# One preLN GFNet + GEGLU kernel: Newton steps for up to four blocks at a time, block 15 folded on VectorE, and another list for the first stage

## The chip, the cores and the metric

The kernel runs on one core of a Trainium2 chip. The metric is the device time of one execution in microseconds (us), as the median of several runs.

## The reference

```python
def reference(A_x, A_w_r, A_w_i, B_x, B_w_gate, B_w_up, B_w_down):
    x = A_x                                            # 1 x 2048 x 512
    h = x + irfft2(rfft2(layernorm(x)) * (A_w_r + 1j * A_w_i))
    n = layernorm(h)
    return h + (gelu(n @ B_w_gate) * (n @ B_w_up)) @ B_w_down   # 512 -> 1376 -> 512
```

`layernorm` subtracts the mean over the last axis and divides by sqrt(variance + 1e-5). `A_w_r` and `A_w_i` are 2048 x 257. Everything is float32.

## The kernel before, in words

The 2048 rows are held as 16 blocks of 128 partitions x 512 columns, in the tile `gh`. The work goes in stages: a first stage of the Fourier transform over the rows, a second stage (transform over the columns, multiplication by `w`, and the first part of the way back), the end of the inverse transform with the second layer norm, and then the gated products, which take most of the time. All run on one core, and every engine takes its instructions in the order in which they are queued.

The change lies in the first stage. For every block b it does this, and the letters are those of the list `START`, which gives the order on each engine:

- `s`, `g`: mean and variance by bn_stats and bn_aggr on VectorE; for some odd blocks `m`, `q` instead, mean and sum of squares on ScalarE.
- `r`: rs = 1/sqrt(var + eps) by a ScalarE table. Beside it VectorE writes var + eps into the scratch `tmp`, which lies in PSUM.
- `n`: one Newton step on `rs`, three small VectorE instructions.
- `c`: ScalarE scales the block's cosine and sine table `mfs` by `rs` into `ms`. So the norm's division goes into the weights of the matmuls.
- `f`: GpSimd folds the columns of a group of one or two blocks: difference and sum of the two halves of a row, into `pn`, two instructions.
- `v` (`fold2`) and `u` (`sums2`): differences `uv` and sums `us` of the halves of `pn`. Where a block has no `u`, TensorE adds its two halves by one more matmul for each.
- `a`, `b`: `transform`, the matmuls of the block: components 0 and 1 from `pn` or `us`, components 2 and 3 from `uv`. An f32 matmul shows as two TensorE instructions.
- `k`, `l`: the block's spectrum is copied from PSUM to `ts`, by ScalarE or, for half of block 15, by VectorE.

Blocks are grouped as in `GROUPS`: 0 and 1 alone, six pairs, 14 and 15 alone. `r` and `n` go by group, but 14 and 15 together. Block 15's `f`, `u` and `v` are on GpSimd (`ON_POOL`). Fourteen small matmuls ahead of the stage warm TensorE up.

The second stage (`SECOND`) begins with `over_d`, whose matmuls (L413) read all 16 blocks of `ts`, so that it cannot begin before the first stage's last copy. Its other steps are `filtered` (multiplication by `w`) and `back`. The sums and differences `wh` of the edge columns of `w` are made on GpSimd and scaled by ScalarE; `patch_w` puts them into the tiles of `w`. `prep` prepares the gate and up weights (L199 and what follows) and its first GpSimd instruction waits for the last VectorE `fold2` (`lasts`).

The order of each engine inside one list is that of the list. Instructions of different lists (such as the edge sums, which stand behind `START` in the text) are put in order by a planner that runs when the kernel is built, by what it takes to be ready; `tc.issue_after(kept.ins)` names `kept`, the last ScalarE copy of the first stage, and queues what its block holds behind it.

Of the kernel before, what the change touches and what calls it, by code (L numbers as in the profile page):

```python
# [16 lines left out]
ALU = mybir.AluOpType  # L17
# [3 lines left out]
P = 128  # L21
NB = 16
# [3 lines left out]
EPS = 1e-5  # L26
# [5 lines left out]
BY_THEN = (8, 12, 9)  # L32

START = """
s0 g0 r0 s1 n0 g1 r1 f0 c0 a0 f1 s2 s3 g2 m5 f2 f4 f6 f8 g3 s4 n1 r2 q5 g4 c1 n2 a1 r4 v0 c2 a2 b0 c3 n4 m7 s6 v1 c4
c5 a4 g6 q7 m9 s8 v2 r6 g8 a3 b1 n6 q9 a5 s10 b3 m11 r8 c6 c7 k0 q11 b2 a6 g10 n8 a7 v4 c8 b4 b5 k1 a8 f10 f12 m13 k2
c9 a9 s12 v6 b6 b7 f14 r10 f15 u15 k3 g12 q13 n10 c10 c11 a10 m15 v8 b9 k4 a11 r12 k6 v10 k7 k5 b11 n12 b8 c12 s14 g14
q15 v12 c13 r14 k9 n14 b10 k10 k11 a12 c14 c15 u14 v14 v15 k8 a13 b13 k13 b12 a14 b14 k12 k14 a15 b15 l15 k15
"""

ON_POOL = (15,)

FIRST = """
u0.1 u4.0 w4 C4.0 V4.2 X4 w0 C0.1 V0.3 X0 U1.2 C1.4 V1.0 X1 r0 U5.3 C5.5 V5.1 M4.1 O4.0 M0.2 O0.1 U2.3 H4 H0 X5 C2.5
# [69 lines left out]
def kernel(  # L114
# [16 lines left out]
    pe, act, dve, pool = nc.tensor, nc.scalar, nc.vector, nc.gpsimd  # L131
# [6 lines left out]
    ident = base.tile([P, P], F32, name="ident")  # L138
# [4 lines left out]
    mv = base.tile([P, NB, 2], F32, name="mv")  # L143
# [18 lines left out]

    ps = ctx.enter_context(tc.tile_pool(name="ps", bufs=1, space=PSUM)).tile([P, 8, 512], F32, name="ps")

    for _ in range(14):

        pe.matmul(ps[:, 6, :P], ident, ident, start=True, stop=True)

    k3 = ctx.enter_context(tc.tile_pool(name="k3", bufs=1))
    dis = k3.tile([P, 4, P], F32, name="dis")  # L170
    mis = k3.tile([P, NB, P], F32, name="mis")
# [16 lines left out]
    def load_gu(f, slowly=False, after=None, by=None, raw=None):  # L188

        nonlocal turn  # L190
        t = raw() if raw else wgp.tile([P, 7, 2 * P], F32, name="raw")
        nc.sync.dma_start(t[:, :2], wgu[f, :, :2])
        nc.sync.dma_start(t[:, 3:6:2], wgu[f, :, 2:])
        r = gus[:, turn]
        turn = 1 - turn
        gu[f] = r.rearrange("p h m (c n) -> p h m c n", c=2)
        yield
        with held("late"):
            pooled["raw"] = i = pool.tensor_tensor(t[:, 4], t[:, 0], t[:, 3], op=ALU.subtract)  # L199
        if after:  # L200
            behind(i, after())
        yield
        pool.tensor_tensor(t[:, 3], t[:, 3], t[:, 5], op=ALU.add)
        yield
        pool.tensor_tensor(t[:, 2], t[:, 3], t[:, 0], op=ALU.subtract)
        yield
        pool.tensor_tensor(t[:, 6], t[:, 1], t[:, 2], op=ALU.subtract)
        yield
        if slowly:
            for m in range(7):  # L210
                split(r[:, 0, m], r[:, 1, m], t[:, m], pool)
                yield
        else:
            if not by:
                dve.tensor_copy(r[:, 0], t)  # L215
                yield
            for m in (slice(0, 1), slice(1, 4), slice(4, 7)):
                if by:
                    by.activation(r[:, 0, m], t[:, m], AF.Copy)
                pooled["lo"] = pool.tensor_tensor(r[:, 1, m], t[:, m], r[:, 0, m].bitcast(F32), op=ALU.subtract)  # L220
                yield
# [5 lines left out]
    with (  # L227
# [9 lines left out]
        rs = cp.tile([P, NB], F32, name="rs")  # L237
# [12 lines left out]
        group = {b + i: (b, n) for b, n in GROUPS for i in range(n)}  # L250
# [15 lines left out]
        def load_w(t):  # L266
            wts[t] = wtp.tile([P, 2, 2, NQ], F32, name="wt")
            nc.sync.dma_start(wts[t], w[t])

        ws = cp.tile([P, 2, NT, 2, 2, 2], F32, name="ws")  # L270
# [28 lines left out]
            act.activation(jk, gh[:, b], AF.Square, scale=D**-0.5, bias=m4[:, b : b + 1], accum_out=mv[:, b, 1:])  # L299


        tmp = ps[:, 7].rearrange("p (b k) -> p b k", b=NB)

        def root(b):

            n = group[b][1] if b < 14 else 2
            act.activation(rs[:, b : b + n], mv[:, b : b + n, 1], AF.Abs_reciprocal_sqrt, bias=eps)
            dve.tensor_scalar(tmp[:, b : b + n, 0], mv[:, b : b + n, 1], EPS, None, op0=ALU.add)

        def newton(b):  # L310

            n = group[b][1] if b < 14 else 2
            r, (ve, t) = rs[:, b : b + n], (tmp[:, b : b + n, k] for k in range(2))
            dve.scalar_tensor_tensor(t, r, -0.5, ve, op0=ALU.mult, op1=ALU.mult)
            dve.tensor_tensor(t, t, r, op=ALU.mult)
            dve.scalar_tensor_tensor(r, t, 1.5, r, op0=ALU.add, op1=ALU.mult)

        mss, pns, parts = {}, {}, {b: [None] * 4 for b in range(NB)}
# [5 lines left out]
        def fold(b):  # L324
            n = group[b][1]
            xv = gh[:, b : b + n].rearrange("p b (e n) -> p b e n", e=2)
            pn = pns[b] = w1.tile([P, 2, 2, 2, P], F32, name="pn", bufs=7)[:, :n]
            pv = pn.rearrange("p b e h n -> p b e (h n)")
            pool.tensor_tensor(pv[:, :, 1], xv[:, :, 0], xv[:, :, 1], op=ALU.subtract)  # L329
            pool.tensor_tensor(pv[:, :, 0], xv[:, :, 0], xv[:, :, 1], op=ALU.add)  # L330
            for i in range(n):
                parts[b + i][:2] = [[pn[:, i, 0, 0], pn[:, i, 0, 1]], [pn[:, i, 1, 0], pn[:, i, 1, 1]]]

        def fold2(b):
# [3 lines left out]
            uv = w1.tile([P, 2, 2, P], F32, name="uv", bufs=3)[:, :n]  # L338
            eng = pool if b in ON_POOL else dve
            i = eng.tensor_tensor(uv, pn[:, :, :, 0], pn[:, :, :, 1], op=ALU.subtract)  # L340
# [5 lines left out]
        def sums2(b):  # L346
            pn = pns[group[b][0]][:, b - group[b][0]]
            us = w1.tile([P, 2, P], F32, name="us", bufs=5)
            eng = pool if b in ON_POOL else dve
            eng.tensor_tensor(us, pn[:, :, 0], pn[:, :, 1], op=ALU.add)  # L350
            parts[b][:2] = [[us[:, 0]], [us[:, 1]]]

# [20 lines left out]
        def keep_half(b):  # L373
# [5 lines left out]
            "m": mean,  # L379
            "q": square,  # L380
            "r": root,
            "n": newton,
            "c": scale,
            "f": fold,
            "v": fold2,
            "u": sums2,
            "a": lambda b: transform(b, (0, 1)),
            "b": lambda b: transform(b, (2, 3)),
            "k": keep,
            "l": keep_half,  # L390
        }
        et = mybir.EngineType
        with tc.manual_schedule(engines={et.PE, et.Activation, et.DVE, et.Pool}):
            for op in START.split():
                kept = steps[op[0]](int(op[1:]))
            odd = slice(5, 16, 2)
            dve.tensor_scalar(mv[:, odd, 0], m4[:, odd], -(D**0.5), None, op0=ALU.mult)


# [2 lines left out]
        wh = cp.tile([P, NT, 2, 2, 2], F32, name="wh")  # L402
# [5 lines left out]
        def over_d(t, k):  # L408

            pd = ps[:, k : k + 2]  # L410
            for c, (e, q) in enumerate(((0, 0), (1, 1), (0, 1), (1, 0))):
                o = pd[:, e, q * NQ // 2 : (q + 1) * NQ // 2]
                pe.matmul(o, ts[:, t, c].rearrange("p x b k -> p (x b k)"), dfs[:, c], start=True, stop=True)  # L413
            pdv = pd[:, :, :NQ].rearrange("p e (s q) -> p s e q", s=2)
            dps[t] = w2.tile([P, 2, 2, NQ // 2], F32, name="dp", bufs=5)
            for h, d in ((slice(0, 64), 1), (slice(64, P), -1)):
                act.activation(dps[t][h], pdv[h, ::d], AF.Copy)  # L417
# [42 lines left out]

        with tc.manual_schedule(engines={et.PE, et.Activation, et.DVE, et.Pool}):
            prep = itertools.chain(raw0, load_gu(1, True))
            for m, op in enumerate((ALU.add, ALU.subtract)):
                pool.tensor_tensor(wh[:, :, m], ws[:, 0, :, m], ws[:, 1, :, m], op=op)
            with tc.issue_after(kept.ins):
                act.activation(wh, wh, AF.Copy, scale=0.5)
            for _ in range(4):
                next(prep)
            rounded = 0
            for op in SECOND.split():  # L470
                name, *place = op.split(".")
                t = int(name[1:] or 0)
                if name == "h":
                    for _ in range(2 if rounded == 6 else 1):
                        next(prep, None)
                    rounded += 1
                elif name[0] == "o":
                    over_d(t, int(place[0]))
                elif name[0] == "f":
                    filtered(t)  # L480
                    if t + AHEAD < NT:
                        load_w(t + AHEAD)
                else:
                    (patch_w if name[0] == "p" else back)(t)
# [3 lines left out]
    w3 = ctx.enter_context(tc.tile_pool(name="w3", bufs=2, reuse_waits="tile"))  # L488
# [928 lines left out]
```

## Time and profile before

| | |
|---|---|
| median of 3 runs | 441.16 us (440.86, 441.16, 442.53) |
| the profiled execution | 440.67 us, its span 438.9 us |
| granted TensorE clock | 1.0 throughout |
| busy share of the span | PE 98%, DVE 71%, ACT 55%, POOL 72% |
| busy 10.40 to 30.90 us (20.5) | PE 20.38, DVE 17.19, ACT 19.20, POOL 20.42 us |
| first matmul of `over_d` (L413) | 30.84 us |

In the rows of the profile, times are in us: the start, the length, the engine, the line of the kernel, the operation, what it writes and reads with the shape, and in brackets the idle time of the engine before it with what ended it. The length of an instruction holds any time for which it is blocked once it has begun; waiting for a semaphore ahead of it is idle time. PE is TensorE, PEld its weight loads, DVE is VectorE, ACT is ScalarE, POOL is GpSimd, SP the engine that issues most DMAs. Rows that group instructions give, behind the count, busy us and mean ns, and the idle us before them.

### The profile page before, as it was taken

The page shows a single profiled execution, that of the slowest core. Times are in us where ns is not written, and L with a number is a line of the kernel's source. Part 1 is how long each engine was busy: PE and PEld are TensorE (multiplying, and loading weights), DVE is VectorE, ACT ScalarE, POOL GpSimd, SP SyncE. Part 2 cuts the span into 40 slices and gives each one's busy share as a digit, 9 for nine tenths or more (in the row PEclk, how much of TensorE's full clock was granted, in tenths as well). Part 3 has the DMA queues.
Part 4 walks back from the last instruction along what each step waited for, and adds up shares of the span by engine and source line. Part 5 has one row for each costly group of instructions (what it writes and reads, how often), then busy time and mean ns, then how long its engine had stood idle before and what let it go on. Part 6 is the DMA issues. An engine that isn't in the chain of part 4 may idle for free.

```text
span 438.9 us, 6623 instructions
## 1 busy us (share of the span) xinstructions
PE 430.6 (98%) x2265; PEld 365.9 (83%) x2265; DVE 312.2 (71%) x583; ACT 243.0 (55%) x505; POOL 316.9 (72%) x350
## 2 busy tenths in 40 slices
PE   6999999999999999999999999999999999999996
PEld 6999999789978777877888888888888888888885
DVE  5968986897864766368734579578677787687785
ACT  4989785799712442124432787376455653565640
POOL 6997896999859788648652945067879779787821
PEclk9999999999999999999999999999999999999999
DMA  8996905320023112112220203401212021200005
GB/s 278 401 410 115 339 16 170 121 72 25 25 96 98 49 50 96 48 48 73 72 73 25 72 25 119 167 8 67 73 49 72 27 70 49 72 25 2 1 0 193
DMA packets 23542, 41.61 MB, mean 95 GB/s; under 512 B 4178, under 2 KB 9810, under 8 KB 23380
## 3 DMA queue, kind: packets, MB, share of 16 engines
q1 hardware_dynamic: 23364, 41.05, 27.5%
q8 instruction: 18, 0.29, 0.3%
q10 hardware_dynamic: 144, 0.13, 0.1%
q14 instruction: 16, 0.13, 0.1%
HBM read 36.97 MB, written 4.20 MB: 94 GB/s over the span
## 4 chain that ended last, share of the span: by engine, by line
PE 89%; POOL 4%; DVE 3%; issue 2%; DMA 1%; ACT 1%; DVEq 0%; SPq 0%; POOLq 0%
PE ps L157 15%; PE ps L159 15%; PE ps L158 15%; PE ps L756 14%; PE ps L1095 11%; PE ps L413 3%; PE ps L424 3%; PE ps L451 3%; PE ps L517 3%; PE ps L856 2%; PE ps L964 1%; POOL pn L330 1%; PE ps L1201 1%; POOL pn L329 1%; DMA gh<-in_x 1%
## 5 line engine op out<-in xcount | busy, mean ns | idle before, releaser
L157 PE MATMUL ps<-cb,gu 128*128 128x512 f32 (+1 forms) x336 | 127.2, 378 | 0.3 <-DVE a L682 0.3
L159 PE MATMUL ps<-cb,gu 128*128 128x512 f32 (+1 forms) x336 | 124.9, 372 | 0.0
L158 PE MATMUL ps<-cb,gu 128*128 128x512 f32 (+1 forms) x336 | 124.9, 372 | 0.0
L660 ACT ACTIVATE s<-ps 128x512 f32<-128x512 f32 (+1 forms) x72 | 40.4, 561 | 86.4 <-PE ps L159 86.0
L220 POOL TENSOR_TENSOR gu<-raw,gu 128x768 fp32r<-128x768 f32 (+1 forms) x42 | 61.3, 1481 | 29.8 <-DVE gu L215 14.1
L157 PEld LDWEIGHTS ps<-cb,gu 128*128 128x128 f32 x336 | 63.3, 188 | 12.2 <-issue 1.0
L158 PEld LDWEIGHTS ps<-cb,gu 128*128 128x128 f32 x336 | 63.3, 188 | 11.7 <-issue 1.0
L159 PEld LDWEIGHTS ps<-cb,gu 128*128 128x128 f32 x336 | 63.3, 188 | 11.0
L756 PE MATMUL ps<-wd,a 128*128 128x512 f32 x264 | 63.6, 393 | 0.0
L756 PEld LDWEIGHTS ps<-wd,a 128*128 128x128 f32 x264 | 49.2, 188 | 11.5 <-DVE gh L965 1.0
L669 DVE TENSOR_TENSOR ps<-ps,s 128x512 f32<-128x512 f32 (+1 forms) x48 | 31.1, 651 | 28.2 <-PE ps L159 25.3
L1102 DVE TENSOR_TENSOR gh<-ps,gh 128x512 f32<-128x512 f32 x66 | 44.2, 680 | 0.8 <-PE ps L1095 0.8
L666 ACT ACTIVATE s<-s 128x512 f32<-128x512 f32 (+1 forms) x48 | 28.4, 593 | 21.1 <-DVE s L663 21.1
L762 DVE TENSOR_TENSOR gh<-ps,gh 128x512 f32<-128x512 f32 x24 | 16.6, 690 | 25.9 <-PE ps L756 25.9
L663 DVE TENSOR_TENSOR s<-ps,s 128x512 f32<-128x512 f32 (+1 forms) x48 | 30.7, 640 | 5.8 <-PE ps L159 4.7
L498 POOL TENSOR_TENSOR wd<-wdr,wd 128x512 fp32r<-128x512 f32 x12 | 15.6, 1299 | 18.3 <-ACT wd L496 18.3
L663 DVE TENSOR_TENSOR ps<-ps,s 128x512 f32<-128x512 f32 (+1 forms) x24 | 15.7, 653 | 15.7 <-ACT s L660 15.2
L675 ACT ACTIVATE a<-ps 128x512 fp32r<-128x512 f32 (+1 forms) x26 | 13.8, 533 | 17.7 <-DVE ps L669 17.7
L1008 POOL TENSOR_TENSOR t<-mis,t 128x768 fp32r<-128x768 f32 (+1 forms) x9 | 13.3, 1482 | 13.2 <-ACT t L1006 13.2
L417 ACT ACTIVATE dp<-ps 64x520 f32<-64x520 f32 x32 | 19.1, 597 | 3.8 <-PE ps L413 3.3
L199 POOL TENSOR_TENSOR raw<-raw 128x256 f32<-128x256 f32 x16 | 11.8, 740 | 12.7 <-DMA raw<-in_wgu 12.7
L440 POOL TENSOR_TENSOR z<-t,t 128x520 f32<-128x520 f32 x15 | 19.5, 1297 | 1.0 <-DVE t L432 0.9
(182 smaller groups left out, 897.5 us busy)
## 6 DMA issues: line engine op xcount, KB each, us to landing
wt<-in_w SPq DMA_DIRECT2D x16, 520.0 KB, 7.6
raw<-in_wgu SPq DMA_DIRECT2D x32, 256.0 KB, 3.0
out<-gh SPq DMA_DIRECT2D x15, 256.0 KB, 2.0
gh<-in_x SPq DMA_DIRECT2D x7, 512.0 KB, 8.9
row<-in_x SPq DMA_DIRECT2D x12, 256.0 KB, 2.8
wdr<-in_wd SPq DMA_DIRECT2D x12, 256.0 KB, 2.5
mis<-in_wd SPq DMA_DIRECT2D x10, 256.0 KB, 2.5
a<-in_wgu SPq DMA_DIRECT2D x8, 256.0 KB, 3.1
```

Of the source, the lines that this page charges most:

```text
L157: pe.matmul(o, lh, rh, start=(i == 0 and not onto), stop=False, skip_group_check=True)
L158: pe.matmul(o, lh, rl, start=False, stop=False, skip_group_check=True)
L159: last = pe.matmul(o, ll, rh, start=False, stop=(i == n - 1), skip_group_check=True)
L220: pooled["lo"] = pool.tensor_tensor(r[:, 1, m], t[:, m], r[:, 0, m].bitcast(F32), op=ALU.subtract)
L440: eng.tensor_tensor(z[:, :, first], t1[:, :, first], t2[:, :, first], op=ALU.add)
L660: return lambda: act.activation(to, a, AF.Copy)
L663: return lambda: dve.tensor_tensor(to, a, b, op=ALU.add)
L666: return lambda: act.activation(g, g, AF.Gelu_apprx_tanh)
L669: return lambda: dve.tensor_tensor(u, u, g, op=ALU.mult)
L756: pe.matmul(o, parts_of[tiles.index((0, f))][:, ha, i // 4, r], wds[f][:, hw, c], start=start, stop=stop)
L1095: pe.matmul(ps[:, k], w[:, hw], a[ha], start=start and hw + ha == 0, stop=hw == 1, skip_group_check=True)
L1102: by.tensor_tensor(to, o, to, op=ALU.add)
```

## The change

- A root and a Newton step are made once for blocks 0, 1, 2 to 3, 4 to 7, 8 to 11 and 12 to 15 (`ROOTS`). The instruction that wrote var + eps into PSUM is gone; the Newton step is still three instructions, and its first now reads the variance from `mv` and the root from `rs` and does both the addition and the product.
- Block 15 is folded on VectorE (`ON_VECTOR`), and its `u` and `v` are there too; the new list also has a `u` for block 13.
- Block 3's statistics are made by ScalarE, block 15's by VectorE; `odd`, a later correction of the means, follows this.
- The GpSimd sums of the edges of `w` are written inside the block that is queued behind `kept`.
- `START` is another list for TensorE, ScalarE, VectorE and GpSimd, with a new letter `w`: small matmuls like those of the warm-up, three at a time, at two places early in TensorE's queue.

```diff
@@ -32,13 +32,19 @@
 BY_THEN = (8, 12, 9)
 
 START = """
-s0 g0 r0 s1 n0 g1 r1 f0 c0 a0 f1 s2 s3 g2 m5 f2 f4 f6 f8 g3 s4 n1 r2 q5 g4 c1 n2 a1 r4 v0 c2 a2 b0 c3 n4 m7 s6 v1 c4
-c5 a4 g6 q7 m9 s8 v2 r6 g8 a3 b1 n6 q9 a5 s10 b3 m11 r8 c6 c7 k0 q11 b2 a6 g10 n8 a7 v4 c8 b4 b5 k1 a8 f10 f12 m13 k2
-c9 a9 s12 v6 b6 b7 f14 r10 f15 u15 k3 g12 q13 n10 c10 c11 a10 m15 v8 b9 k4 a11 r12 k6 v10 k7 k5 b11 n12 b8 c12 s14 g14
-q15 v12 c13 r14 k9 n14 b10 k10 k11 a12 c14 c15 u14 v14 v15 k8 a13 b13 k13 b12 a14 b14 k12 k14 a15 b15 l15 k15
+s0 g0 f0 f1 r0 n0 c0 m3 s1 g1 r1 s2 q3 m5 f2 g2 r2 v0 n1 a0 w3 b0 w3 v1 n2 c1 q5 s4 s6 a1 b1 c2 g6 a2 m7 c3 a3 f4 g4
+v2 f6 q7 r4 b3 n4 v4 m9 c4 c5 s8 g8 b2 c6 s10 g10 q9 a4 m11 a5 b5 f8 b4 f10 c7 v6 a6 k0 a7 q11 r8 k4 k1 n8 c8 v8 k3
+s12 c9 c10 s15 b7 s14 g14 k2 f12 f14 m13 b6 g12 g15 c11 a8 b8 q13 a9 b9 k9 v10 k5 r12 a10 k8 n12 a11 b11 v12 c12 c13
+b10 k10 a12 b12 k6 k7 u13 a13 c14 c15 k12 u14 f15 b13 k13 k11 v14 a14 b14 u15 a15 v15 b15 k14 l15 k15
 """
 
-ON_POOL = (15,)
+ON_POOL = ()
+
+ON_VECTOR = (15,)
+
+SUMS_ON_POOL = ()
+
+ROOTS = {0: 1, 1: 1, 2: 2, 4: 4, 8: 4, 12: 4}
 
 FIRST = """
 u0.1 u4.0 w4 C4.0 V4.2 X4 w0 C0.1 V0.3 X0 U1.2 C1.4 V1.0 X1 r0 U5.3 C5.5 V5.1 M4.1 O4.0 M0.2 O0.1 U2.3 H4 H0 X5 C2.5
@@ -162,10 +168,12 @@
 
     ps = ctx.enter_context(tc.tile_pool(name="ps", bufs=1, space=PSUM)).tile([P, 8, 512], F32, name="ps")
 
-    for _ in range(14):
-
-        pe.matmul(ps[:, 6, :P], ident, ident, start=True, stop=True)
-
+    def keep_warm(n):
+
+        for _ in range(n):
+            pe.matmul(ps[:, 6, :P], ident, ident, start=True, stop=True)
+
+    keep_warm(14)
     k3 = ctx.enter_context(tc.tile_pool(name="k3", bufs=1))
     dis = k3.tile([P, 4, P], F32, name="dis")
     mis = k3.tile([P, NB, P], F32, name="mis")
@@ -299,20 +307,19 @@
             act.activation(jk, gh[:, b], AF.Square, scale=D**-0.5, bias=m4[:, b : b + 1], accum_out=mv[:, b, 1:])
 
 
-        tmp = ps[:, 7].rearrange("p (b k) -> p b k", b=NB)
+        tmp = ps[:, 7, :NB]
 
         def root(b):
 
-            n = group[b][1] if b < 14 else 2
+            n = ROOTS[b]
             act.activation(rs[:, b : b + n], mv[:, b : b + n, 1], AF.Abs_reciprocal_sqrt, bias=eps)
-            dve.tensor_scalar(tmp[:, b : b + n, 0], mv[:, b : b + n, 1], EPS, None, op0=ALU.add)
 
         def newton(b):
 
-            n = group[b][1] if b < 14 else 2
-            r, (ve, t) = rs[:, b : b + n], (tmp[:, b : b + n, k] for k in range(2))
-            dve.scalar_tensor_tensor(t, r, -0.5, ve, op0=ALU.mult, op1=ALU.mult)
-            dve.tensor_tensor(t, t, r, op=ALU.mult)
+            n = ROOTS[b]
+            r, t = rs[:, b : b + n], tmp[:, b : b + n]
+            dve.scalar_tensor_tensor(t, mv[:, b : b + n, 1], EPS, r, op0=ALU.add, op1=ALU.mult)
+            dve.scalar_tensor_tensor(t, t, -0.5, r, op0=ALU.mult, op1=ALU.mult)
             dve.scalar_tensor_tensor(r, t, 1.5, r, op0=ALU.add, op1=ALU.mult)
 
         mss, pns, parts = {}, {}, {b: [None] * 4 for b in range(NB)}
@@ -326,8 +333,9 @@
             xv = gh[:, b : b + n].rearrange("p b (e n) -> p b e n", e=2)
             pn = pns[b] = w1.tile([P, 2, 2, 2, P], F32, name="pn", bufs=7)[:, :n]
             pv = pn.rearrange("p b e h n -> p b e (h n)")
-            pool.tensor_tensor(pv[:, :, 1], xv[:, :, 0], xv[:, :, 1], op=ALU.subtract)
-            pool.tensor_tensor(pv[:, :, 0], xv[:, :, 0], xv[:, :, 1], op=ALU.add)
+            eng = dve if b in ON_VECTOR else pool
+            eng.tensor_tensor(pv[:, :, 1], xv[:, :, 0], xv[:, :, 1], op=ALU.subtract)
+            eng.tensor_tensor(pv[:, :, 0], xv[:, :, 0], xv[:, :, 1], op=ALU.add)
             for i in range(n):
                 parts[b + i][:2] = [[pn[:, i, 0, 0], pn[:, i, 0, 1]], [pn[:, i, 1, 0], pn[:, i, 1, 1]]]
 
@@ -346,7 +354,7 @@
         def sums2(b):
             pn = pns[group[b][0]][:, b - group[b][0]]
             us = w1.tile([P, 2, P], F32, name="us", bufs=5)
-            eng = pool if b in ON_POOL else dve
+            eng = pool if b in SUMS_ON_POOL else dve
             eng.tensor_tensor(us, pn[:, :, 0], pn[:, :, 1], op=ALU.add)
             parts[b][:2] = [[us[:, 0]], [us[:, 1]]]
 
@@ -388,12 +396,13 @@
             "b": lambda b: transform(b, (2, 3)),
             "k": keep,
             "l": keep_half,
+            "w": keep_warm,
         }
         et = mybir.EngineType
         with tc.manual_schedule(engines={et.PE, et.Activation, et.DVE, et.Pool}):
             for op in START.split():
                 kept = steps[op[0]](int(op[1:]))
-            odd = slice(5, 16, 2)
+            odd = slice(3, 14, 2)
             dve.tensor_scalar(mv[:, odd, 0], m4[:, odd], -(D**0.5), None, op0=ALU.mult)
 
 
@@ -460,9 +469,9 @@
 
         with tc.manual_schedule(engines={et.PE, et.Activation, et.DVE, et.Pool}):
             prep = itertools.chain(raw0, load_gu(1, True))
-            for m, op in enumerate((ALU.add, ALU.subtract)):
-                pool.tensor_tensor(wh[:, :, m], ws[:, 0, :, m], ws[:, 1, :, m], op=op)
             with tc.issue_after(kept.ins):
+                for m, op in enumerate((ALU.add, ALU.subtract)):
+                    pool.tensor_tensor(wh[:, :, m], ws[:, 0, :, m], ws[:, 1, :, m], op=op)
                 act.activation(wh, wh, AF.Copy, scale=0.5)
             for _ in range(4):
                 next(prep)
```

## The prediction

> **What bounds the kernel now.** I read the page first (the span and the chain that ended last), then the stretches of the first stage, then each engine's instructions there in order of time.
>
> ```profile
> span 438.9 us, 6623 instructions
> PE 89%; POOL 4%; DVE 3%; issue 2%; DMA 1%; ACT 1%; DVEq 0%; SPq 0%; POOLq 0%
> 7.80:10.40 2.60, 1.15 (x9) 0.99 (x9) 2.40 (x13) 2.08 (x7) 2.60 (x3) 1.00 1.02 384
> 10.40:30.90 20.50, 20.38 (x177) 19.92 (x177) 17.19 (x47) 19.20 (x55) 20.42 (x20) 1.00 1.03 405
> ```
>
> TensorE carries 89% of the chain. The two stretches give, after their length, the busy time of PE, PEld, DVE, ACT and POOL. From 10.40 to 30.90 us PE and POOL are full, ACT is at 94% and DVE at 84%: whoever loses a microsecond there hands it to PE. Behind this stage PE takes up `over_d` without a break:
>
> ```profile
> 1.37 5.60 PE L167 MATMUL ps<-ident 128*128 128x128 f32 x28 [1.37 <-POOL ident masks.py:199]
> 10.38 2.02 PE L363 MATMUL ps<-ms,pn 128*128 128x128 f32 x16 [1.45 <-ACT ms L322]
> 12.68 1.95 PE L363 MATMUL ps<-ms,pn 128*128 128x128 f32 x16
> 14.47 0.61 PE L363 MATMUL ps<-ms,uv 128*128 128x128 f32 x4
> 30.17 0.71 PE L363 MATMUL ps<-ms,uv 128*128 128x128 f32 x4
> 30.84 0.35 PE L413 MATMUL ps<-dfs,ts 128*128 128x130 f32 x1
> 30.31 0.43 DVE L374 COPY ts<-ps 128x256 f32<-128x256 f32 x1 [2.01 <-PE ps L363]
> ```
>
> So the date to forecast is when L413 starts, 30.84 us now. Everything behind it hangs on PE or on chains released by it, and I carry a shift of that date one to one to the end. Sixteen PE instructions take 14.47 - 12.68 = 1.79 us, 0.112 us each. The row at 12.68 is blocks 4 and 3, so block 4 begins at 12.68.
>
> **The tiny VectorE instructions.**
>
> ```profile
> 9.97 0.17 DVE L314 SCALAR_TENSOR_TENSOR ps<-rs,ps 128x2 f32<-128x2 f32 x1
> 10.37 0.16 DVE L316 SCALAR_TENSOR_TENSOR rs<-ps,rs 128x2 f32<-128x2 f32 x1
> L308 DVE TENSOR_SCALAR ps<-mv 128x2 f32<-128x2 f32 (+1 forms) x9 | 1.4, 156 | 0.2
> ```
>
> A Newton step costs three dependent instructions 0.20 us apart (first and last are shown), and the root adds one of 0.156 us. Nine groups make 36 such instructions; the new code has six groups of three, 18. At about 0.16 us that removes 18 x 0.16 = 2.9 us of VectorE time, and three of the nine ACT roots.
>
> But look at the operands. Today each of them has at most one input in SBUF; the scratch `tmp` is in PSUM. The new first instruction reads `mv` and `rs`, both in SBUF. What two SBUF inputs cost beside GpSimd is shown by the sums `uv` and `us`, and by one instruction as small as ours:
>
> ```profile
> 8.43 1.27 POOL L330 TENSOR_TENSOR pn<-gh 128x512 f32<-128x512 f32 x1
> 10.88 1.45 POOL L330 TENSOR_TENSOR pn<-gh 128x512 f32<-128x512 f32 x1
> 12.29 1.47 POOL L329 TENSOR_TENSOR pn<-gh 128x512 f32<-128x512 f32 x1
> 13.72 1.72 POOL L330 TENSOR_TENSOR pn<-gh 128x512 f32<-128x512 f32 x1
> 10.71 0.49 DVE L340 TENSOR_TENSOR uv<-pn 128x256 f32<-128x256 f32 x1
> 13.21 1.10 DVE L340 TENSOR_TENSOR uv<-pn 128x512 f32<-128x512 f32 x1
> 26.52 0.90 DVE L350 TENSOR_TENSOR us<-pn 128x256 f32<-128x256 f32 x1
> 27.34 0.95 DVE L340 TENSOR_TENSOR uv<-pn 128x256 f32<-128x256 f32 x1
> 27.10 0.91 POOL L330 TENSOR_TENSOR pn<-gh 128x256 f32<-128x256 f32 x1
> 71.62 0.73 POOL L438 TENSOR_TENSOR z<-t,t 128x260 f32<-128x260 f32 x1
> 71.64 0.73 DVE L441 TENSOR_TENSOR z<-z 128x2 f32<-128x2 f32 x1
> ```
>
> The `uv` at 13.21 takes 1.10 us and ends at 14.31, 0.55 us after the fold before it ends (12.29 + 1.47 = 13.76). The fold behind it takes 1.72 instead of 1.27: 0.45 lost. A one-block sum, like the one at 10.71, I put at half the time, 0.29, and at 0.2 lost for the fold behind it (1.45 for 1.27). At 26.52 and 27.34 two VectorE sums stand back to back; GpSimd still gets in between, and the second waits out the fold until 28.01. Decisive is the last row: two elements per partition, 0.73 us, ending at 72.37, as GpSimd's L438, begun 0.02 us earlier, ends at 72.35. Small size doesn't help; it waits for the whole GpSimd instruction.
>
> No row shows a scalar_tensor_tensor with two SBUF inputs beside a running fold. Its bounds are 0.17 us (L314 as it is) and a whole fold, about 1.25, more. I take the wait, since L441 has the same two sources and nearly the same size.
>
> The Trainium skill, "SBUF — State Buffer", section "SBUF: two separate sides", says that a VectorE instruction with two SBUF inputs and a GpSimd instruction exclude each other for the whole instruction, whichever began first. That would put a scalar_tensor_tensor under the same wait; L441's 0.73 us agrees, and for the new instruction itself no row here shows it.
>
> **The new list, walked.** In the new START the steps on VectorE run s0 g0 n0 s1 g1 s2 g2 v0 n1 v1 n2 s4 s6 g6 g4 v2 n4 v4 s8 g8 s10 g10 v6 n8 v8. So n1, n2, n4 and n8 each stand right behind a `v`, which itself was let in as a fold ended. The next fold starts as `v` leaves, and `n` meets it at its start: the worst place.
>
> ```profile
> 7.20 1.27 POOL L329 TENSOR_TENSOR pn<-gh 128x512 f32<-128x512 f32 x1
> 7.14 1.28 DVE L286 BATCH_NORM_STATS2 bn<-gh 128x6 f32<-128x512 f32 x2
> 8.33 0.30 DVE L289 BATCH_NORM_AGGREGATE mv<-bn 128x2 f32<-128x6 f32 x2
> 26.92 0.69 ACT L322 ACTIVATE ms<-mfs,rs 128x128 f32<-128x128 f32 x2
> L294 ACT ACTIVATE jk<-gh 128x512 f32<-128x512 f32 x6 | 3.7, 620 | 0.7 <-DMA gh<-in_x 0.7
> L299 ACT ACTIVATE jk<-gh,m 128x512 f32<-128x512 f32 x6 | 4.3, 710 | 0.0
> L307 ACT ACTIVATE rs<-mv,eps 128x2 f32<-128x2 f32 (+1 forms) x9 | 2.6, 286 | 4.1 <-DVE mv L289 4.1
> ```
>
> A free half fold takes 8.43 - 7.20 = 1.23 us, a statistic 0.60, a merge 0.15, and a scale 0.4 until its result is there.
> - Fold 2 runs 7.20 to 8.43 as now. v0 asks at about 7.9, gets 8.43. The second half runs 8.63 to 9.86; n1 asks at 8.7 and gets 9.86, done 10.46.
> - Fold 4 from 9.95 (the tiny one holds it 0.1) to 11.18: v1 asks 10.46, gets 11.18, leaves 11.47. The next half runs to 12.60: n2 asks 11.47, gets 12.60, done 13.20.
> - s4, s6 and two merges reach 14.7. Fold 6's halves run 12.70 to 13.93 and 13.93 to 15.16; v2 gets 15.16. Fold 8 from 15.62 to 16.85: n4 asks 15.72, gets 16.85, done 17.45. Scale 4 is there at 17.85, so block 4 begins on PE at about 17.9, against 12.68 now.
> - fold 8's second half 16.95 to 18.18, v4 to 18.74, four small steps to 20.2; v6 gets 21.10 (end of fold 10); fold 12 from 21.56 to 22.79; n8 gets 22.79, done 23.4; block 8 begins on PE at 23.9.
>
> PE has 12 instructions per block, 8 where `u` has made the sums (now also block 13). Blocks 4 to 7 are 48 x 0.112 = 5.4 us, 17.9 to 23.3; 0.6 idle until 23.9; blocks 8 to 12 and 13 to 15 are 60 + 24 = 84, 9.4 us, to 33.3. Block 15's first half ends 0.45 earlier, and its copy (0.43, row L374) with two handovers of 0.1 lets L413 start at about 33.4. That is 33.4 - 30.84 = **2.6 us later**. The bound from block 4 alone, without the stop at block 8, is 2.0.
>
> **The other parts.**
>
> ```profile
> 26.41 0.73 POOL L329 TENSOR_TENSOR pn<-gh 128x256 f32<-128x256 f32 x1
> 27.98 0.77 POOL L464 TENSOR_TENSOR wh<-ws 128x64 f32<-128x64 f32 x2
> 28.71 0.72 POOL L350 TENSOR_TENSOR us<-pn 128x256 f32<-128x256 f32 x1
> 29.40 0.72 POOL L340 TENSOR_TENSOR uv<-pn 128x256 f32<-128x256 f32 x1
> 30.08 0.72 POOL L199 TENSOR_TENSOR raw<-raw 128x256 f32<-128x256 f32 x1
> 30.92 0.38 ACT L371 ACTIVATE ts<-ps 128x256 f32<-128x256 f32 x1 [0.92 <-PE ps L363]
> 31.20 0.30 ACT L466 ACTIVATE wh<-wh 128x128 f32<-128x128 f32 x1
> 32.11 2.44 ACT L417 ACTIVATE dp<-ps 64x520 f32<-64x520 f32 x4
> ```
>
> Fold 15 and its sums leave POOL (26.41 to 28.71 less the edge sums, and 28.71 to 30.08, some 3 us) and become two folds, u15, v15 on VectorE, with u13 six short instructions of 0.29 to 0.45 us. By the walk VectorE comes to n12 at about 28, then to these at 29.2, and ends v15 at 31.2, over a microsecond before PE wants it (32.3), with POOL idle since 26.4. So today's tail, where PE waited for POOL's 29.40, is gone, but hidden behind PE's backlog: nothing. Without that backlog it is worth the 1.0 us of the first rival.
>
> Roots of four make c4 wait for q7. On ACT r4 stands behind c2, m7, c3 and q7; counted from n2's 13.2 by the L322, L294, L299 and L307 rows, with 0.2 for the accumulator's reading, that is 0.4 + 0.6 + 0.3 + 0.9 + 0.3 = 2.5, ready at 15.7, when n4 asks: no further cost. The three-matmul `w3` fillers and the earlier block 0 lie in PE's idle time before block 1. Block 13's `u` saves 4 x 0.112 = 0.45, counted above.
>
> The edge sums `wh` stand in a block named after `kept`, an ACT instruction. Today they ran at 27.98, between fold 15 and u15, ahead of list order, so GpSimd takes them when it is free. I take them at 26 us, before VectorE's last sums, for nothing. If they do wait for `kept`, ACT's L466 waits 0.77 + 0.1 more, and with it gu, p0 and the dp copies that feed PE: 0 to 0.9. The raw preparation L199 waits for the last `v` (31.2 against 28.3): 1.2 us later than 30.08, less than the stage's 2.6, so covered. No DMA moves in its queue.
>
> **Sum.** The profiled execution took 440.67 us, 0.49 under the median of 441.16. 440.67 + 2.6 = 443.3; on the median's scale 443.8.
>
> **The rivals.**
> - *The short instruction doesn't wait.* Then the list dovetails. PE begins block 0 at about 7.0, behind the warm-up (1.37 + 5.60), with 180 + 12 instructions x 0.112 = 21.5 us, to 28.5; with the 0.8 of gaps it has today after 10.4 us (from 10.38 to 30.84 less 176 x 0.112) and 0.5 for block 15's copy, L413 starts at 29.8: 1.0 earlier, 440.2. Not slower; it decides if the new L314 stays under 0.2 us beside folds. For it: the 2.9 us off VectorE. Against: L441. The Trainium skill, "VectorE: DVE Perf Modes", section "Rules for kernel authors", advises keeping the number of chained VectorE operations low, which would give this gain; L441's 0.73 us for one operation says that count alone isn't the cost here.
> - *It waits, but meets folds halfway.* Half of the 3.6 us between the two cases: +0.8, 442.0. For it: v0's place hangs on when blocks 2 and 3 land. Against: each `n` follows its `v` directly, as at 27.34.
> - *The edge sums wait for `kept` too*: 2.6 + 0.9 = +3.5, 444.7. The cut-in at 27.98 speaks against it.
>
> **How the numbers follow.** Forecast 0.70, no wait 0.13, halfway 0.09, edge sums 0.08. A measurement tells about 0.5%, 2.2 us: below 438.95 is faster, above 443.37 slower. The forecast's own range is 442.8 to 444.7 (from the bound of 2.0 and the runs' spread). A quarter of it, 0.17, falls within 0.5%, with no wait (0.13, of which 0.02 faster by luck of my sum), halfway 0.09 and 0.01 of the last: 0.38 same, 0.60 slower, 0.02 faster. The range 441.8 to 445.0 leaves out the no-wait case, a third of halfway and the top: 0.2.
>
> **What would show it.** In the changed profile the first Newton instruction's mean should be near 0.9 us (six of them, four near 1.2), block 4's matmuls start near 17.9, block 8's near 23.9, L413 (by its new line) near 33.4, POOL's folds end before 26.5. I am wrong if the short instructions keep 0.16 us, or if PE starts block 4 before 15 us, or if `wh` follows `kept`.

## The result, and the profile after

The changed kernel takes 443.7 us (median of 6 runs, 443.63 to 444.83) against 441.01 us of the kernel before (median of 6). The ratio is 1.0062, with a 95% interval of 1.0044 to 1.008: slower by 2.7 us. The prediction was 443.8 us, slower.

First the page of the changed kernel: its span and the chain that ended last, by engine; then one row of its stretches.

```profile
span 441.5 us, 6605 instructions
...
PE 90%; DVE 5%; POOL 1%; issue 1%; ACT 1%; DMA 1%; DVEq 0%; POOLq 0%
```

```profile
10.40:30.90 20.50, 17.76 (x148) 17.04 (x149) 19.17 (x39) 16.66 (x46) 15.70 (x14) 1.00 1.03 405
```

The last row is the same stretch of the first stage as before: busy time of PE, PEld, DVE, ACT and POOL. PE has lost 2.62 us of busy time (20.38 to 17.76), GpSimd 4.72 and ScalarE 2.54; only VectorE has gained, 17.19 to 19.17. The change took instructions off VectorE, and VectorE became the engine that the others wait for. Its first Newton instruction is now L321. VectorE's instructions in order of time (start, duration in us, in brackets the idle time before), then the group of this line, then two of GpSimd's in order of time:

```profile
7.83 0.94 DVE L348 TENSOR_TENSOR uv<-pn 128x256 f32<-128x256 f32 x1
...
8.70 1.23 DVE L321 SCALAR_TENSOR_TENSOR ps<-mv,rs 128x1 f32<-128x1 f32 x1
...
11.33 1.23 DVE L321 SCALAR_TENSOR_TENSOR ps<-mv,rs 128x2 f32<-128x2 f32 x1
...
15.46 1.23 DVE L321 SCALAR_TENSOR_TENSOR ps<-mv,rs 128x4 f32<-128x4 f32 x1
...
21.28 1.24 DVE L321 SCALAR_TENSOR_TENSOR ps<-mv,rs 128x4 f32<-128x4 f32 x1
...
27.90 0.17 DVE L321 SCALAR_TENSOR_TENSOR ps<-mv,rs 128x4 f32<-128x4 f32 x1 [0.91 <-ACT rs L315]
```

```profile
L321 DVE SCALAR_TENSOR_TENSOR ps<-mv,rs 128x4 f32<-128x4 f32 (+2 forms) x6 | 5.3, 884 | 1.3 <-ACT rs L315 1.3
```

```profile
8.45 1.45 POOL L338 TENSOR_TENSOR pn<-gh 128x512 f32<-128x512 f32 x1
...
25.50 0.59 POOL L474 TENSOR_TENSOR wh<-ws 128x64 f32<-128x64 f32 x2
```

Four times it takes 1.23 or 1.24 us, with one, two or four elements per partition. The one at 8.70 ends at 9.93, and the fold L338 that stood beside it ends at 9.90. The sixth, at 27.90, is its own control: GpSimd has nothing left after 26.09 (the edge sums at 25.50), and the same instruction in the same shape takes 0.17 us.

What that does to the others is in the waits of the first 36 us (who waited for whom: us in all, times, longest), in PE's instructions in order of time, and in one row of the chain that ended last:

```profile
ACT ms L329 <- DVE rs L323: 5.2, 6, 1.5
...
PE ps L371 <- ACT ms L329: 3.5, 5, 1.1
```

```profile
17.67 2.02 PE L371 MATMUL ps<-ms,pn 128*128 128x128 f32 x16 [0.92 <-ACT ms L329]
...
33.95 2.92 PE L422 MATMUL ps<-dfs,ts 128*128 128x130 f32 x24 [0.60 <-ACT ts L379]
```

```profile
23.50 9.88 PE ps L371 x84
```

ScalarE waited 5.2 us for Newton steps, and PE 3.5 us for ScalarE's scales. Block 4 begins on PE at 17.67 (12.68 before). Not all of these 5 us are the wait: the old list has block 4 ahead of block 3 and of the second halves of blocks 1 and 2, and with the new list without the wait it begins at 15.30 (the third experiment). Block 8 begins at 23.50; from there PE works off its 84 instructions in one piece, and `over_d` (now L422) starts at 33.95 instead of 30.84.

### The profile page after: what moved, and what is told of

Read it like the earlier page. It is cut to its first block, busy times and chain, and to the rows that moved or that the text cites. A ratio compares the mean times of both kernels' runs of the same rounds, so it can differ in the third digit from the quotient of the medians.

```text
span 441.5 us, 6605 instructions
## 1 busy us (share of the span) xinstructions
PE 431.7 (98%) x2273; PEld 366.4 (83%) x2273; DVE 315.4 (71%) x570; ACT 243.1 (55%) x502; POOL 312.8 (71%) x346
## 4 chain that ended last, share of the span: by engine, by line
PE 90%; DVE 5%; POOL 1%; issue 1%; ACT 1%; DMA 1%; DVEq 0%; POOLq 0%
PE ps L163 15%; PE ps L165 15%; PE ps L164 15%; PE ps L765 14%; PE ps L1104 11%; PE ps L422 3%; PE ps L433 3%; PE ps L460 3%; PE ps L526 3%; PE ps L371 2%; PE ps L865 2%; PE ps L973 1%; DVE ps L321 1%; DVE uv L348 1%; PE ps L1210 1%
## 5 line engine op out<-in xcount | busy, mean ns | idle before, releaser
L507 POOL TENSOR_TENSOR wd<-wdr,wd 128x512 fp32r<-128x512 f32 x12 | 15.5, 1290 | 18.8 <-ACT wd L505 18.8
L1017 POOL TENSOR_TENSOR t<-mis,t 128x768 fp32r<-128x768 f32 (+1 forms) x9 | 13.3, 1481 | 13.2 <-ACT t L1015 13.2
```

## The experiments

The theory is that of the prediction: the new first Newton instruction reads two operands from SBUF and therefore waits until GpSimd's running fold has ended. The rivals are the new order of the list, and the roots of four blocks. Each kernel was timed together with the kernel before, whose median in these runs was 441.55 to 441.76 us; the ratios are to it.

**Old arithmetic, everything else changed.** L315 to L323 go back to the old form:

```diff
+            dve.tensor_scalar(tmp[:, b : b + n, 0], mv[:, b : b + n, 1], EPS, None, op0=ALU.add)
...
-            dve.scalar_tensor_tensor(t, mv[:, b : b + n, 1], EPS, r, op0=ALU.add, op1=ALU.mult)
-            dve.scalar_tensor_tensor(t, t, -0.5, r, op0=ALU.mult, op1=ALU.mult)
...
+            dve.scalar_tensor_tensor(t, r, -0.5, ve, op0=ALU.mult, op1=ALU.mult)
+            dve.tensor_tensor(t, t, r, op=ALU.mult)
```

> The changed kernel with the old root and Newton arithmetic (var + eps into PSUM by one VectorE instruction, then three with at most one SBUF input each), everything else as changed: list, groups of four, block 15 on VectorE. Theory (the two-SBUF first Newton instruction waits out folds): no small VectorE instruction above 0.2 us, block 4 on PE near 13.5 us, over_d near 30.5 us instead of 33.95, time 440 to 441 us, that is 3 us under the changed kernel and at or a little under the kernel before. Rival one (the new order of the list is the cost): block 4 stays near 17.7 and the time near 443.7. Rival two (roots of four blocks hold the scales up): the same, with ScalarE waiting for VectorE's statistics ahead of the roots.

```profile
L322 DVE SCALAR_TENSOR_TENSOR ps<-rs,ps 128x4 f32<-128x4 f32 (+2 forms) x6 | 1.0, 162 | 1.9 <-ACT rs L315 1.8
```

```profile
15.71 2.02 PE L372 MATMUL ps<-ms,pn 128*128 128x128 f32 x16
...
30.97 2.92 PE L423 MATMUL ps<-dfs,ts 128*128 128x130 f32 x24 [0.18 <-ACT ts L380]
```

Ratio 1.0005 (0.9993 to 1.0017): the whole loss is gone with six more VectorE instructions. Block 4 came at 15.71 and not at 13.5 as expected, and `over_d` at 30.97 instead of 30.5, so no gain of the rest of the change shows, where up to 1 us was expected.

**The new arithmetic alone, in the kernel before.** Old list, nine groups, block 15 on GpSimd; only the arithmetic is the new one.

```diff
-            dve.tensor_scalar(tmp[:, b : b + n, 0], mv[:, b : b + n, 1], EPS, None, op0=ALU.add)
...
-            dve.scalar_tensor_tensor(t, r, -0.5, ve, op0=ALU.mult, op1=ALU.mult)
-            dve.tensor_tensor(t, t, r, op=ALU.mult)
...
+            dve.scalar_tensor_tensor(t, mv[:, b : b + n, 1], EPS, r, op0=ALU.add, op1=ALU.mult)
+            dve.scalar_tensor_tensor(t, t, -0.5, r, op0=ALU.mult, op1=ALU.mult)
```

> The kernel before with nothing changed but the Newton arithmetic: no var + eps in PSUM, three instructions, the first with the variance and the root both from SBUF; old list, old nine groups. Theory: its first Newton instruction is seen at lengths up to 1.25 us beside folds, PE falls behind as in the changed kernel, over_d 2 to 4 us later than 30.84, time 443 to 445 us. Both rivals (order, groups of four): nine instructions fewer on VectorE, so the time is 441.0 or up to 0.5 us lower.

```profile
L313 DVE SCALAR_TENSOR_TENSOR ps<-mv,rs 128x2 f32<-128x2 f32 (+1 forms) x9 | 6.3, 695 | 0.8 <-ACT rs L307 0.7
```

```profile
7.88 1.13 PE L362 MATMUL ps<-ms,pn 128*128 128x128 f32 x8 [1.46 <-ACT ms L321]
...
10.96 3.27 PE L362 MATMUL ps<-ms,pn 128*128 128x128 f32 x16 [1.95 <-ACT ms L321]
...
33.50 2.70 PE L412 MATMUL ps<-dfs,ts 128*128 128x130 f32 x22 [0.18 <-ACT ts L370]
```

```profile
12.60:14.20 1.60, 1.60 (x9) 1.60 (x9) 1.53 (x5) 0.34 (x2) 1.60 (x2) 0.50 1.02 420
```

Ratio 1.0035 (1.0022 to 1.0048): with nothing of the list, the groups or block 15 changed, the arithmetic alone makes the kernel slower. `over_d` moved by 2.7 us. But part of that is a second thing that I had not expected: behind PE's gaps sixteen instructions took 3.27 us instead of 2.02, and the granted clock from 12.60 to 14.20 us is 0.50 (in the stretch's row, the figure behind the five busy times). More on that below. The wait costs without it too, as far as one execution shows: of the five, one ran at a mean granted clock of 0.999, and it took 443.22 us, more than all 21 executions of the kernel before that ran at 0.998 or more beside it (440.84 to 442.34).

**Three instructions, one SBUF input each.** ScalarE writes the root into the PSUM scratch, and the intermediate goes to SBUF:

```diff
-            act.activation(rs[:, b : b + n], mv[:, b : b + n, 1], AF.Abs_reciprocal_sqrt, bias=eps)
+            act.activation(tmp[:, b : b + n], mv[:, b : b + n, 1], AF.Abs_reciprocal_sqrt, bias=eps)
...
-            r, t = rs[:, b : b + n], tmp[:, b : b + n]
+            r, t = tmp[:, b : b + n], half[:, b : b + n]
...
-            dve.scalar_tensor_tensor(r, t, 1.5, r, op0=ALU.add, op1=ALU.mult)
+            dve.scalar_tensor_tensor(rs[:, b : b + n], t, 1.5, r, op0=ALU.add, op1=ALU.mult)
```

> The changed kernel, but ScalarE writes the root into the PSUM scratch, and the Newton step's intermediate goes to a small SBUF tile: still three VectorE instructions for each of six groups, now each with one input in SBUF and one in PSUM. Theory: all of them near 0.17 us, block 4 on PE near 13.2, over_d near 29.9 to 30.3, time 439.8 to 440.8 us: under both kernels. Rivals (order of the list, groups of four): near 443.7, as in the changed kernel.

```profile
L322 DVE SCALAR_TENSOR_TENSOR half<-mv,ps 128x4 f32<-128x4 f32 (+2 forms) x6 | 0.9, 155 | 2.6 <-ACT ps L316 2.6
```

```profile
9.52 0.16 DVE L322 SCALAR_TENSOR_TENSOR half<-mv,ps 128x1 f32<-128x1 f32 x1 [0.81 <-ACT ps L316]
...
14.18 0.16 DVE L322 SCALAR_TENSOR_TENSOR half<-mv,ps 128x4 f32<-128x4 f32 x1
```

```profile
10.63 1.13 PE L372 MATMUL ps<-ms,pn 128*128 128x128 f32 x8 [0.42 <-ACT ms L330]
...
14.31 1.16 PE L372 MATMUL ps<-ms,uv 128*128 128x128 f32 x8
...
15.30 2.02 PE L372 MATMUL ps<-ms,pn 128*128 128x128 f32 x16
...
30.56 2.92 PE L423 MATMUL ps<-dfs,ts 128*128 128x130 f32 x24 [0.18 <-ACT ts L380]
```

Ratio 0.999 (0.9981 to 0.9999): the same operation, the same count and list as the changed kernel, and 884 ns have become 155. This settles it between theory and rivals: what made the changed kernel slower is where the operand lies. Block 4 came at 15.30 and `over_d` at 30.56, later than expected (13.2, and 29.9 to 30.3). PE hardly idles ahead of block 4: its eight instructions from 14.31 end their turn at 14.31 + 8 x 0.112 = 15.2. It is late because block 1 begins only at 10.63.

**Shorter folds.** The changed kernel, with a pair folded one block at a time:

```diff
-            eng.tensor_tensor(pv[:, :, 1], xv[:, :, 0], xv[:, :, 1], op=ALU.subtract)
-            eng.tensor_tensor(pv[:, :, 0], xv[:, :, 0], xv[:, :, 1], op=ALU.add)
+            for i in range(n):
+                eng.tensor_tensor(pv[:, i, 1], xv[:, i, 0], xv[:, i, 1], op=ALU.subtract)
+                eng.tensor_tensor(pv[:, i, 0], xv[:, i, 0], xv[:, i, 1], op=ALU.add)
```

> The changed kernel, with GpSimd's folds of a pair made one block at a time: four instructions of 0.69 us instead of two of 1.23, 0.3 us more GpSimd time for each of six pairs. Theory (the wait is what is left of the fold in progress): the first Newton instruction's mean falls from 0.88 to about 0.55 us, block 4 on PE from 17.7 to near 15.5, over_d from 33.95 to 32 to 33, time 442 to 443 us, in spite of 1.7 us more work for GpSimd. Rivals: the mean stays near 0.88 us, and more GpSimd work makes the time 443.7 or longer.

```profile
L321 DVE SCALAR_TENSOR_TENSOR ps<-mv,rs 128x4 f32<-128x4 f32 (+2 forms) x6 | 2.8, 467 | 1.0 <-ACT rs L315 1.0
```

```profile
7.97 0.69 DVE L321 SCALAR_TENSOR_TENSOR ps<-mv,rs 128x1 f32<-128x1 f32 x1
```

```profile
14.41 2.02 PE L372 MATMUL ps<-ms,pn 128*128 128x128 f32 x16 [0.28 <-ACT ms L329]
...
32.15 2.92 PE L423 MATMUL ps<-dfs,ts 128*128 128x130 f32 x24 [0.60 <-ACT ts L380]
```

Ratio 1.0008 (0.9998 to 1.0017). More work for GpSimd, and the kernel is 0.5% faster than the changed one: the wait is as long as what is left of the fold, 467 ns in the mean instead of 884, and 0.69 us at most (the one at 7.97). Block 4 came at 14.41, earlier than expected (15.5) and than without any wait of the Newton step (15.30): VectorE's sums, which wait for the same folds, took less too (the first one 0.39 us, 0.94 in the changed kernel). So the gain in time is not the Newton instruction's alone.

**A root moved by one place.** In the kernel with the root in PSUM, n1 idled 0.81 us for the next root, which writes the same scratch (the row at 9.52 above).

```diff
-... f2 g2 r2 v0 n1 a0 ...
+... f2 g2 v0 n1 r2 a0 ...
```

> The kernel with the root in PSUM, and in the list the root of blocks 2 and 3 moved from ahead of v0 to behind n1 (ScalarE's own order stays the same). There n1 sat idle 0.81 us on VectorE until ScalarE's next root, which writes the same PSUM scratch, was done. Theory: that idle goes, block 1 and 2 begin about 0.8 us earlier, block 4 on PE near 14.4 instead of 15.30, over_d near 29.7 instead of 30.56, time 0.7 to 1.3 us under the kernel before. Rival (ScalarE or the loads of x set block 4): block 4 stays near 15.3 and the time about 0.4 us under the kernel before, as with the root in PSUM alone.

```profile
14.64 2.01 PE L372 MATMUL ps<-ms,pn 128*128 128x128 f32 x16
...
30.69 2.92 PE L423 MATMUL ps<-dfs,ts 128*128 128x130 f32 x24 [0.18 <-issue]
```

```profile
19.35 1.75 DVE L349 TENSOR_TENSOR uv<-pn 128x512 f32<-128x512 f32 x1 [0.61 <-PE ps L372]
```

n1's idle time is gone and block 4 came 0.66 us earlier (0.9 expected), but block 1 only 0.1 (10.53), `over_d` not at all, and the ratio stayed at 0.999 (0.9982 to 0.9998). The gain was lost again on the way. Block 8's sums `v8`, the last row, started at 19.35, as they did with the root ahead of `v0` (19.34). The row names PE, but the matmuls that read the buffer which these sums overwrite (blocks 2 and 3) had ended by 14.81. What ended just ahead of them, at 19.31, is GpSimd's fold of blocks 8 and 9, which they read; there it had ended at 18.30. GpSimd was late in this execution from the start: the load of block 2 let it begin that block's fold at 7.70 instead of 7.15. Whether another order of the list, or an execution without the late load, keeps the gain is open.

**One copy on VectorE.** On top of that, block 11's PSUM copy goes from ScalarE to VectorE, behind v15.

```diff
-... k13 k11 v14 a14 b14 u15 a15 v15 b15 k14 l15 k15
+... k13 v14 a14 b14 u15 a15 v15 d11 b15 k14 l15 k15
...
+            "d": lambda b: dve.tensor_copy(*kept_of(b, slice(0, 4))),
```

> The same as e5_root_two_behind, and the PSUM copy of block 11, one of the last four of ScalarE ahead of over_d, made by VectorE behind v15, where VectorE is idle. Theory (at the end of the stage over_d waits for ScalarE's row of copies): one copy of 0.48 us leaves that row, over_d starts 0.2 to 0.5 us earlier than in e5_root_two_behind, the time falls by as much. Rival (over_d waits for block 15's second half on PE alone): no change.

```profile
29.47 0.61 PE L372 MATMUL ps<-ms,uv 128*128 128x128 f32 x4
...
30.68 2.92 PE L424 MATMUL ps<-dfs,ts 128*128 128x130 f32 x24 [0.59 <-ACT ts L380]
```

```profile
30.15 0.42 DVE L383 COPY ts<-ps 128x256 f32<-128x256 f32 x1 [0.46 <-PE ps L372]
```

No change: ratio 1.0 (0.9989 to 1.0011). PE's last matmuls came 0.42 us earlier than with only the root moved (29.47 instead of 29.89), but `over_d` again starts 0.1 us behind the copy of block 15's first half (30.15 + 0.42). That copy began as PE's last matmuls ended (29.47 + 0.61), 0.52 us behind the matmuls that it reads (29.02 + 0.61); with only the root moved it began 0.1 us behind them. Why it paused is open.

**The edge sums really held.** In the changed kernel they ran at 25.50, so the block they stand in doesn't hold GpSimd back. Here a dependency makes them wait for the last copy:

```diff
-                    pool.tensor_tensor(wh[:, :, m], ws[:, 0, :, m], ws[:, 1, :, m], op=op)
+                    behind(pool.tensor_tensor(wh[:, :, m], ws[:, 0, :, m], ws[:, 1, :, m], op=op), kept)
```

> The changed kernel, with GpSimd's edge sums made to wait for the last ScalarE copy of the first stage, as the block they stand in suggests; in the changed kernel they ran at 25.5 us, without that wait. If what stands behind them on ScalarE is exposed, over_d still starts near 33.95, the first copies dp come 0.9 us later (near 36.0), and the time is 0.4 to 0.9 us over the changed kernel, near 444.4. If PE has enough queued, the time stays at 443.7.

```profile
33.69 0.60 POOL L474 TENSOR_TENSOR wh<-ws 128x64 f32<-128x64 f32 x2 [8.31 <-ACT ts L379]
```

```profile
35.25 2.42 ACT L426 ACTIVATE dp<-ps 64x520 f32<-64x520 f32 x4
```

Ratio 1.0057 (1.0045 to 1.0069), not told apart from the changed kernel's 1.0062. ScalarE waits 0.71 us for the edge sums, and the copies dp start 1.48 us behind `over_d` (35.25 and 33.77) instead of 1.17 (35.12 and 33.95). So 0.3 of the 0.9 us shows there, and nothing in the time.

**The better arithmetic in the kernel before.** Old list, old groups; the three instructions of the kernel with the root in PSUM:

```diff
-            act.activation(rs[:, b : b + n], mv[:, b : b + n, 1], AF.Abs_reciprocal_sqrt, bias=eps)
-            dve.tensor_scalar(tmp[:, b : b + n, 0], mv[:, b : b + n, 1], EPS, None, op0=ALU.add)
+            act.activation(tmp[:, b : b + n], mv[:, b : b + n, 1], AF.Abs_reciprocal_sqrt, bias=eps)
...
+            r, t = tmp[:, b : b + n], half[:, b : b + n]
+            dve.scalar_tensor_tensor(t, mv[:, b : b + n, 1], EPS, r, op0=ALU.add, op1=ALU.mult)
...
```

> The kernel before, old list and groups, with only the Newton arithmetic of e3_root_in_psum: root written to PSUM, three instructions with one SBUF input each, var + eps gone: nine VectorE instructions fewer. Theory (without the port, the saved instructions lie beside a full PE and GpSimd): over_d between 30.4 and 30.9, time 0 to 0.5 us under the kernel before. Rival (VectorE's instruction count set the pace): over_d 1 us or more earlier, time 1 us under the kernel before.

```profile
10.64 2.63 PE L363 MATMUL ps<-ms,pn 128*128 128x128 f32 x16 [2.28 <-ACT ps L308]
...
32.34 1.92 PE L413 MATMUL ps<-dfs,ts 128*128 128x130 f32 x15 [0.18 <-issue]
```

```profile
12.00:13.20 1.20, 1.20 (x7) 1.20 (x7) 1.20 (x4) 1.20 (x5) 1.20 (x1) 0.50 0.98 352
```

A miss: ratio 1.002 (1.0004 to 1.0035), slower, with `over_d` 1.5 us late. Again PE stood idle, 2.28 us, and then ran at a granted clock of 0.50. That accounts for the loss: 9 of the 12 executions had a mean granted clock of 0.996 or less (median 442.64 us); the other three, at 0.998 or more, took 441.07 in the median, 0.3 us less than the kernel before at such a clock (441.36), as the theory said.

**Fillers taken out, and fillers put in.** The changed kernel without its two `w3`, and the last kernel with nine such matmuls (`w9`, from the same helper) in the 2.28 us gap:

```diff
-... a0 w3 b0 w3 v1 ...
+... a0 b0 v1 ...
```

> The changed kernel without its six filler matmuls (the two w3 of the list); nothing waits for them. By the prediction they lie in idle time and do nothing: time 443.7 as in the changed kernel. By the other reading (behind gaps of 1.95 and 2.28 us the two kernels with the old list ran sixteen matmul instructions in 3.27 and 2.63 us instead of 1.95 to 2.02, so a PE left idle runs slowly afterwards): the first sixteen pn instructions after 13 us take 2.6 to 3.3 us instead of 2.02. Since block 4 comes only at 17.67, that may still be hidden: time 443.7 to 444.7.

```diff
-... r1 f0 c0 a0 f1 ...
+... r1 f0 c0 a0 w9 f1 ...
```

> e8_before_root_in_psum with nine filler matmuls behind block 0's first, in the 2.28 us in which PE sat idle. If a PE left idle runs slowly afterwards: the sixteen instructions behind the gap take 1.95 to 2.05 us instead of 2.63, the next sixteen too instead of 2.61, over_d starts 1.0 to 1.4 us earlier than 32.34, the time falls by as much, from 1.002 of the kernel before to about 0.999 to 1.000. If the slow matmuls had another cause, they stay slow and the time stays at 1.002 or goes up.

The first block of rows is of the kernel without fillers, the second of the one with nine.

```profile
8.87 0.71 PE L371 MATMUL ps<-ms,uv 128*128 128x128 f32 x4 [0.81 <-DVE uv L348]
...
10.94 1.13 PE L371 MATMUL ps<-ms,pn 128*128 128x128 f32 x8 [1.36 <-ACT ms L329]
...
34.01 2.25 PE L422 MATMUL ps<-dfs,ts 128*128 128x130 f32 x18 [0.60 <-ACT ts L379]
```

```profile
10.89 2.02 PE L366 MATMUL ps<-ms,pn 128*128 128x128 f32 x16 [0.21 <-ACT ps L311]
...
13.20 1.95 PE L366 MATMUL ps<-ms,pn 128*128 128x128 f32 x16
...
30.96 2.92 PE L417 MATMUL ps<-dfs,ts 128*128 128x130 f32 x24
```

Without fillers the changed kernel stays at 1.0062 (1.0049 to 1.0075), `over_d` at 34.01: its gaps of 0.81 and 1.36 us don't slow PE in the profiled execution, and the fillers do nothing there. With fillers the other kernel's sixteen instructions take 2.02 us instead of 2.63, the next 1.95 instead of 2.61, `over_d` starts 1.38 us earlier, and the ratio falls from 1.002 to 0.9989 (0.9981 to 0.9998); none of its 11 executions had a mean clock below 0.998. So the slow matmuls came from the gap.

No version goes further than 0.1% under the kernel before; three (root in PSUM with the new list, with the root moved, and with the old list and fillers) reach that, with intervals that end just below 1. Part of even this is the clock: these three never ran at a mean clock below 0.998, the kernel before did in 22 of 75 executions. Against its others (441.36 to 441.42 us in the median) they gain 0.2 us.

## Why the prediction was right

- **The waits.** Foreseen: mean near 0.9 us, four near 1.2. Measured: 0.884, four at 1.23 to 1.24. The inference from two elements of a tensor_tensor (0.73 us beside a fold) to a scalar_tensor_tensor held; that the place of the operand is the cause is shown by the two kernels that moved it, and by short folds.
- **The walk.** Block 4 at 17.9 foreseen, 17.67 measured; block 8 at 23.9, 23.50; PE's last four instructions of the stage end their turn at 32.75 + 4 x 0.112 = 33.2, 33.3 foreseen; VectorE's last sum ends at 31.4, 31.2 foreseen; edge sums at 26, 25.50.
- **The term that was mis-sized** is the last handover of the sum, the copy of block 15's first half. It was to follow block 15's first matmuls by 0.1 and let L422 start at 33.4 (the terms add up to 33.48). These matmuls ended at 32.30 + 0.61 = 32.91, but the copy started at 33.43, and `over_d` at 33.95, 0.55 later than foreseen. The first two rows are of the changed kernel, then come VectorE's last groups, of the changed kernel and of the kernel before:

```profile
32.30 0.61 PE L371 MATMUL ps<-ms,us 128*128 128x128 f32 x4
...
33.43 0.42 DVE L382 COPY ts<-ps 128x256 f32<-128x256 f32 x1 [2.01 <-ACT ts L379]
```

```profile
437.02 1.35 DVE L1215 TENSOR_TENSOR gh<-ps,gh 128x512 f32<-128x512 f32 x3 [0.67 <-PE ps L1210]
```

```profile
434.09 1.35 DVE L1206 TENSOR_TENSOR gh<-ps,gh 128x512 f32<-128x512 f32 x3 [0.67 <-PE ps L1201]
```

  Why the copy paused is open. Its row names ScalarE, whose copy of block 14 ended at 33.37. But with the old arithmetic the same copy began 0.1 us behind its matmuls, at 30.45, and block 14's copy ended only at 30.80. With the short folds, and with block 11's copy on VectorE, it paused by 0.5 us again, and block 14's copy had ended 0.3 us ahead of it.

- **One to one to the end.** The 3.11 us at `over_d` are 2.93 at VectorE's last group (437.02, 434.09 before), and 2.6 in the span; from the end of that group to the end of the span it is 3.1 us, 3.5 before. So the tail gave back 0.5. The medians differ by 2.69, and 2.6 was foreseen: that it fits so closely is luck. Block 8 came 0.4 early, the 84 instructions took 9.7 us instead of 9.4, `over_d` was still 0.55 late, and the tail gave that back. What held is the mechanism and the size of the waits.
- **The first rival's price was wrong**, though the rival was. Without the wait the list was to bring `over_d` to 29.8 and the time 1.0 under before. The kernels without it start `over_d` at 30.97, 30.56 and 30.69, with ratios of 1.0005 and 0.999. The step that failed is counting PE's instructions from 7.0 with the gaps of the kernel before: by the count block 1 begins at 7.0 + 24 x 0.112 = 9.7 (behind block 0 and the fillers), but it began at 11.33, 10.63 and 10.53.
- **The third rival's price**, 0.9 for the edge sums, is 0.3 at dp and nothing measurable in the time.
- **Moving block 15 to VectorE** and the fillers were put at nothing. For the fillers that is shown by taking them out; block 15 was never moved by itself, and the kernels that undo the arithmetic show only that it brings no 1 us.

## What to carry to other kernels

Count an instruction not only by its length but by what it may have to wait for: a VectorE instruction of 0.17 us with both inputs in SBUF took up to 1.24 us here, a whole GpSimd instruction, and putting one operand in PSUM took that away without another instruction. Fusing two small instructions into one was worth nothing here, since the fused one reads two operands from SBUF and neither of the two did. Place such an instruction's neighbours with care: right behind another one that was let in between two GpSimd instructions, it met the next one near its start, four times.

## What the runs showed of the hardware that was not expected

PE was granted half its clock within the first stage once it had idled for 1.95 us (after 1.46 us of idling and 1.13 us of work) or 2.28 us: 0.50 from 11.70 to 15.12 us and from 11.88 to 15.29, 3.4 us each time, and 2.6 to 3.3 us for sixteen instructions that otherwise take 1.95 to 2.02. In the profiled executions a gap of 1.45 us in the kernel before, and gaps of up to 1.36 us in the kernel without fillers, left it at 1.00. But the length of the gap doesn't decide it alone. A span with 3.4 us at half clock has a mean clock of 0.996, and 22 of the 75 executions of the kernel before that were timed beside the experiments had 0.994 to 0.996 and took 442.07 to 442.48 us in the median, 0.7 to 1.1 more than the others. The Trainium skill's page "TensorE: Matmul & The Clock Gate", section "Part 1: The HAM clock gate (the "warmup" mystery)", describes a gate that halves the clock by how busy PE was in free-running windows of about 3.4 us; the 0.50 and the 3.4 us agree, while the gaps that sufficed here were shorter than 3.4 us. Why some executions of one kernel are hit and others not, no run here shows.

The small instruction's wait is bounded by the GpSimd instruction, not by its own size: 1.23 us for one, two and four elements per partition alike beside whole folds, and at most 0.69 beside folds of half the size.
